# Token loads ahead of stores, a third block convolved on TensorE, and a softmax on eight partitions, in a causal convolution followed by a GELU feed-forward layer

## The chip, the cores and the metric

The kernel runs on one core of one Trainium2 chip. The metric is the device time of that core in microseconds (us), the median of several executions. All other times are taken from one execution recorded by the hardware profiler, counted from the start of its span.

The engines are named as in the profile: PE (TensorE, matrix multiplication; PEld is its loading of weights), DVE (VectorE), ACT (ScalarE), POOL (GpSimd) and SP (SyncE, which here only issues DMA).

## The reference

Two steps are computed one after the other. First a causal convolution of 7 taps along the sequence, with softmaxed taps, one set for each of 8 heads of 24 channels; then a feed-forward layer with an exact GELU.

```python
# x: (8, 4096, 192); weight: (8, 7); w_in: (192, 2048); w_out: (2048, 192)
w = softmax(weight, axis=-1)                      # max subtracted, 1e-9 added to the sum
x_pad = concatenate([zeros((B, 6, D)), x], axis=1)
x_unf = x_pad[:, idx, :].reshape(B, S, 7, 8, 24)  # 7 shifted copies
conv = einsum('hk,bskhg->bshg', w, x_unf).reshape(B * S, 192)
h = conv @ w_in
out = (0.5 * h * (1 + erf(h / sqrt(2)))) @ w_out  # (32768, 192), float32
```

## The kernel before

The 32768 tokens are split into two halves of 16384. Partitions 0 to 63 hold 64 channels of a token of the first half, partitions 64 to 127 the same channels of a token of the second half; `NP` = 3 parts p make up the 192 channels. A block n is `WS[n]` tokens of each half: four blocks of 256 and thirty of 512, so `NB` = 34.

A block passes through these stages:

- **Load** (`load`, L171): four DMAs (q = 0 to 3) bring fp32 tokens into one of three buffers `xin`. A buffer is reused only when all transposes of the block that used it are done (`S_TR`). 380 KB a DMA for a block of 512, 188 KB for one of 256.
- **Transpose** (`trans`, L396) on DVE, into `xT`, which is used in turn by even and odd blocks. POOL (`halo`, L289, L300, L306) adds the tokens that lie ahead of the block.
- **Convolution.** For blocks 2 and up it is done on DVE (`conv`, L419 and L426): 7 taps for each of 3 parts, 21 operations. For the first `ND` = 2 blocks it is done on PE (`pconv`, L575): the tokens are cast to bf16 in `xTb`, then multiplied with 7 diagonal matrices `dg` (made by `diag`, L357), 14 small matmuls a part, into PSUM at the place that `CONVB` names. The result is copied to `xc` by ACT for block 0 (L501) and by DVE for block 1 (`conv_out`, L382).
- **Expansion** `mm1` (L611) on PE, into `hp`, in 8 slices (block of 256) or 16 slices (block of 512); the GELU (L522) on ACT follows each slice.
- **Contraction** `mm2` (L643) on PE into `ob`. Its units for block n-1 are laid between the slices of `mm1` of block n, in equal shares. With 256 tokens a block has 2 groups g, with 512 it has 4; a group has 32 units.
- **Eviction** `evac` (L435) on DVE, from `ob` to `osb`, one for each group, and **store** (L185, L208) by SP.

PE's order is written out by hand (L659 to L679): in block 0 the list `behind` puts extra work behind slices, the three remaining `dup` (which mirror `w_in` into the other half of the partitions, through PE and a DVE copy, L367) and then the three parts of `pconv(1)`. Block n may begin `mm1` only when `xc` is complete (`S_PCE` for the blocks convolved on PE, `S_CV` for the others).

DVE's order is written out too: softmax and diagonals, `trans(0)`, copies of `dup`, `trans(1)`, its casts and copies, and from block 2 on 24 operations a block: 3 transposes, then 21 convolution operations. The table `late` tells ahead of which operation each eviction is placed: `(1, 1): (4, 6)` is group 1 of block 1, ahead of operation 6 of block 4.

SP's queue is in order (L682 to L696): weights of the convolution, loads of blocks 0 to 2 (block 1 only after the first part of `w_in` is there), a wait for `w_out`, then in turn `load(n + 2)` and `store(n - 1)`. A store waits for the evictions of its block, so the load behind it in the queue waits with it.

The softmax (L316 to L352) is computed on all 128 partitions with a broadcast copy of the weights: reduce, subtract on DVE, Exp on ACT, then sum, add, reciprocal, multiply on DVE, and a product with the mask `msk` (made by POOL) and a reduction, which give `wcol`, the tap of each partition. PE meanwhile runs 22 matmuls on zeros (L535), to keep busy until the first data are there.

Of the kernel before, what the change touches and what calls it, by code (L numbers as in the profile page):

```python
# [5 lines left out]
ALU = mybir.AluOpType  # L6
# [5 lines left out]
def bass_lightweight_conv__then__act_gelu_exact_kernel(  # L12
# [21 lines left out]
    ND = 2  # L34
# [54 lines left out]
    with es:  # L89
        win = sbt("win", [128, NP * F], BF16)  # L90
        wout = sbt("wout", [128, NF * C], BF16)
        wsb = sbt("wsb", [128, H * KS], F32)
        wmx = sbt("wmx", [128, H], F32)
        wsm = sbt("wsm", [128, H], F32)
        wrc = sbt("wrc", [128, H], F32)
        wex = sbt("wex", [128, H * KS], F32)
        wnm = sbt("wnm", [128, H * KS], F32)
        msk = sbt("msk", [128, NP * H], F32)
        wpr = sbt("wpr", [128, NP * KS * H], F32)
        wcol = sbt("wcol", [128, NP * KS], F32)  # L100
        idn = sbt("idn", [128, 64], F32)
# [3 lines left out]
        hot = sbt("hot", [128, 2], F32)  # L105
# [15 lines left out]
        S_MSK = sem("S_MSK")  # L121
        S_IDN = sem("S_IDN")
        S_WARM = sem("S_WARM")
# [22 lines left out]
        CONVB = [(ob[0], 0), (ob[0], 512), (ob[1], 0)]  # L146
# [18 lines left out]
        def load(e, n, qs=(0, 1, 2, 3)):  # L165
            mb = WS[n] // 32
            if n >= NX:
                e.wait_ge(S_TR, NP * (n - NX + 1))
            for q in qs:
                off = ((q // 2) * HALF + OFF[n]) * D + 32 * (q % 2)  # L170
                e.dma_start(  # L171
                    ap(
                        xin[n % NX],
                        32 * q * (TB // 32 * D),
                        [[TB // 32 * D, 32], [1, mb * D - 32]],
                    ),
                    ap(xt, off, [[mb * D, 32], [1, mb * D - 32]]),
                ).then_inc(S_XIN[n % NX], 16)
# [43 lines left out]
        def _(g):  # L222
# [8 lines left out]

            g.memset(msk[:, :], 1.0).then_inc(S_MSK)
            g.memset(idn[:, :], 1.0).then_inc(S_MSK)
            g.wait_ge(S_MSK, 2)
            for hf in range(2):
                m = msk[64 * hf : 64 * hf + 64, :]
                g.affine_select(
                    out=m,
                    in_=m,
                    compare_op=ALU.is_ge,  # L240
                    fill=0.0,
                    base=0,
                    pattern=[[64, NP], [-GRP, H]],
                    channel_multiplier=1,
                ).then_inc(S_MSK)
            g.wait_ge(S_MSK, 4)
            for hf in range(2):
                m = msk[64 * hf : 64 * hf + 64, :]
                g.affine_select(
                    out=m,  # L250
                    in_=m,
                    compare_op=ALU.is_ge,
                    fill=0.0,
                    base=GRP - 1,
                    pattern=[[-64, NP], [GRP, H]],
                    channel_multiplier=-1,
                ).then_inc(S_MSK)
            for hf in range(2):
                m = idn[64 * hf : 64 * hf + 64, :]
                g.affine_select(  # L260
                    out=m,
                    in_=m,
                    compare_op=ALU.is_equal,
                    fill=0.0,
                    base=0,
                    pattern=[[-1, 64]],
                    channel_multiplier=1,
                ).then_inc(S_IDN)
            g.wait_ge(S_IDN, 2)
            g.tensor_copy(idb[:, :], idn[:, :]).then_inc(S_IDN)  # L270
# [39 lines left out]

            for n in range(NB):
                halo(n)

        @block.vector
        def _(v):
            v.memset(warm[:, :], 0.0).then_inc(S_WARM)  # L316
            hk = [[H * KS, 128], [KS, H], [1, KS]]
            v.wait_ge(S_WSB, 16)
            v.tensor_reduce(  # L319
                wmx[:, :], ap(wsb, 0, hk), mybir.AxisListType.X, ALU.max, negate=True  # L320
            ).then_inc(S_PRO)
            v.wait_ge(S_PRO, 1)
            v.tensor_tensor(
                ap(wex, 0, hk), ap(wsb, 0, hk), ap(wmx, 0, [[H, 128], [1, H], [0, KS]]), ALU.add
            ).then_inc(S_PRO)
            v.wait_ge(S_ACTP, 2)
            v.tensor_reduce(
                wsm[:, :], ap(wnm, 0, hk), mybir.AxisListType.X, ALU.add
            ).then_inc(S_PRO)
            v.wait_ge(S_PRO, 3)  # L330
            v.tensor_scalar(wsm[:, :], wsm[:, :], 1e-9, None, ALU.add).then_inc(S_PRO)
            v.wait_ge(S_PRO, 4)
            v.reciprocal(wrc[:, :], wsm[:, :]).then_inc(S_PRO)
            v.wait_ge(S_PRO, 5)
            v.tensor_tensor(
                ap(wex, 0, hk), ap(wnm, 0, hk), ap(wrc, 0, [[H, 128], [1, H], [0, KS]]), ALU.mult
            ).then_inc(S_PRO)
            v.wait_ge(S_PRO, 6)
            v.wait_ge(S_MSK, 6)
            v.tensor_tensor(  # L340
                ap(wpr, 0, [[NP * KS * H, 128], [KS * H, NP], [H, KS], [1, H]]),
                ap(wex, 0, [[H * KS, 128], [0, NP], [1, KS], [KS, H]]),
                ap(msk, 0, [[NP * H, 128], [H, NP], [0, KS], [1, H]]),
                ALU.mult,
            ).then_inc(S_PRO)
            v.wait_ge(S_PRO, 7)
            v.tensor_reduce(
                wcol[:, :],
                ap(wpr, 0, [[NP * KS * H, 128], [H, NP * KS], [1, H]]),
                mybir.AxisListType.X,  # L350
                ALU.add,
            ).then_inc(S_PRO)  # L352
            v.wait_ge(S_PRO, 8)
            v.wait_ge(S_IDN, 3)

            def diag(p):
                v.tensor_tensor(  # L357
                    ap(dg, p * KS * 64, [[NP * KS * 64, 128], [64, KS], [1, 64]]),
                    ap(idn, 0, [[64, 128], [0, KS], [1, 64]]),
                    ap(wcol, p * KS, [[NP * KS, 128], [1, KS], [0, 64]]),  # L360
                    ALU.mult,
                ).then_inc(S_DG)
# [16 lines left out]
            def conv_out(n, p):  # L379
                v.wait_ge(S_PC, NP * n + p + 1)  # L380
                b, o = CONVB[p]
                v.tensor_copy(  # L382
                    xc[n % 2][:, p * TB : p * TB + WS[n]], ap(b, o, [[1024, 128], [1, WS[n]]])
                ).then_inc(S_PCE)
# [65 lines left out]
            for p in range(NP):  # L450
                diag(p)
            for p in range(NP):
                trans(0, p)
            for q in range(3):
                dup_out(q)
            for p in range(NP):
                trans(1, p)
            for p in range(NP):
                cast(1, p)
            dup_out(3)  # L460
            for p in range(NP):
                conv_out(1, p)


            late = {(0, 0): (2, 18), (0, 1): (3, 8), (1, 0): (3, 20), (1, 1): (4, 6)}
            late.update({(2, 0): (4, 13), (2, 1): (4, 21)})
            for n in range(3, NB):
                for g in range(NG[n]):
                    b, o = n + 2, len(ops0) * (g + 1) // (NG[n] - 1)
                    if g == NG[n] - 1:  # L470
                        b, o = n + 3, 0
                    late[n, g] = (b, o)
# [10 lines left out]
        def _(a):  # L483
            a.wait_ge(S_WARM, 1)
            a.activation(out=hot[:, 0:1], in_=warm[:, 0:1], func=AF.Exp).then_inc(S_ACTP)
            load(a, 0, (2, 3))
            a.wait_ge(S_ACTP, 1)
            a.wait_ge(S_PRO, 2)
            a.activation(out=wnm[:, :], in_=wex[:, :], func=AF.Exp).then_inc(S_ACTP)
            a.activation(out=hot[:, 1:2], in_=warm[:, 0:1], func=AF.Gelu).then_inc(S_HOT)  # L490
# [7 lines left out]
            for p in range(NP):  # L498
                a.wait_ge(S_PC, p + 1)
                b, o = CONVB[p]  # L500
# [31 lines left out]
        def _(t):  # L532
            t.wait_ge(S_WARM, 1)
            for i in range(22):
                t.matmul(hp[1][:, 0:512], warm[:, 0:128], warm[:, :])  # L535

            def dup(s):

                if s == 0:
                    t.wait_ge(S_IDN, 3)  # L540
# [18 lines left out]
            def pconv(n, p):  # L559
                w = WS[n]  # L560
                b, o = CONVB[p]
                t.wait_ge(S_CAST, NP * n + p + 1)
                t.wait_ge(S_HALO, HC[n] + 2 + p)
                if n == 0:
                    t.wait_ge(S_DG, p + 1)
                elif p == 0:
                    t.wait_ge(S_DUPE, 3)
                elif p == 2:
                    t.wait_ge(S_DUPE, 4)
                for k in range(KS - 1, -1, -1):  # L570
# [19 lines left out]
            behind = {1: [(dup, 1)], 2: [(dup, 2)], 3: [(dup, 3)]}  # L590
            for p in range(NP):
                behind[4 + p] = [(pconv, 1, p)]
# [28 lines left out]
            def mm2(m, g, ph, i):  # L621
# [4 lines left out]
                if i == 0:  # L626
                    if ph == 0:
                        if gg >= 2:
                            t.wait_ge(S_EV, gg - 1)
                    else:  # L630
# [28 lines left out]
            for n in range(NB):  # L659
                todo = units(n - 1) if n >= 1 else []  # L660
                for i in range(NSL[n]):
                    mm1(n, i)
                    if n == 0:
                        for f, *q in behind.get(i, []):
                            f(*q)

                    i0 = 1 if n == 1 else 0
# [14 lines left out]
        def _(sp):  # L682
            sp.dma_start(wsb[:, :], ap(wt, 0, [[0, 128], [1, H * KS]])).then_inc(S_WSB, 16)
            load(sp, 0, (0, 1))
            sp.wait_ge(S_WIN[0], 32)
            load(sp, 1)
            load(sp, 2)
            sp.wait_ge(S_WOUT, 16)
            for n in range(1, NB):
                if n + 2 < NB:  # L690
                    load(sp, n + 2)
# [33 lines left out]
```

## Time and profile before

| | us |
|---|---|
| time, median of 3 runs | 707.97 |
| lowest and highest | 707.60, 708.12 |
| span of the profiled execution | 706.7 |
| PE busy | 687.9 (97%) |
| PEld busy | 521.2 (74%) |
| DVE busy | 558.5 (79%) |
| ACT busy | 528.4 (75%) |
| POOL busy | 39.0 (6%) |
| PE, `mm1` (L611), 3264 matmuls | 422.1 |
| PE, `mm2` (L643), 8192 matmuls | 426.7 |
| ACT, GELU (L522), 512 instructions | 523.0 |
| DVE, fused convolution operations (L426), 480 into `acc` | 316.9 |

Busy times of matmuls overlap, as matmuls of the two row halves run at the same time, so the rows of PE add up to more than its busy time. A busy share is an average over the whole span; what a stage waits for has to be read from the timeline of that stage. The idle time that a row gives is that of the engine ahead of the instruction, with what released it.

### The profile page before, as it was taken

How to read it: one execution, taken by the hardware profiler on the slowest of the kernel's cores; microseconds unless marked ns; L12 is line 12 of the kernel's file. 1: busy time of each engine (PE TensorE's matmuls, PEld its weight loads, DVE VectorE, ACT ScalarE, POOL GpSimd, SP SyncE). 2: the span in 40 equal slices, each digit the busy share in tenths (PEclk: the TensorE clock that was granted, in tenths of full speed). 3: DMA queues.
4: the chain of work that ended last, by engine and by line, in shares of the span. 5: the costliest groups of instructions: out<-in, count | busy, mean ns of one | idle time of the engine just before them, and what ended most of it. 6: DMA issues, size and time to landing. Idle time of an engine off the chain costs nothing.

```text
span 706.7 us, 25342 instructions
## 1 busy us (share of the span) xinstructions
PE 687.9 (97%) x11586; PEld 521.2 (74%) x11586; DVE 558.5 (79%) x924; ACT 528.4 (75%) x523; POOL 39.0 (6%) x90
## 2 busy tenths in 40 slices
PE   6995999999999999999999999999999999999998
PEld 3784677777777777777777777777777777777777
DVE  3879889888889888888988888988888988888811
ACT  4664977777777777777777777777777777777771
POOL 4100000000000000000000000000000000000000
PEclk9998999999999999999999999999999999999999
DMA  9456345554445554335554444565444555434113
GB/s 185 89 118 152 76 98 136 135 118 95 91 103 136 135 132 101 92 87 129 135 135 99 109 86 113 135 135 129 96 92 91 134 135 135 109 90 89 30 46 92
DMA packets 22795, 78.18 MB, mean 111 GB/s; under 512 B 7072, under 2 KB 10912, under 8 KB 18848
## 3 DMA queue, kind: packets, MB, share of 16 engines
q1 hardware_dynamic: 19056, 74.21, 45.7%
q0 software_dynamic: 2896, 1.57, 1.7%
q8 instruction: 91, 1.49, 1.0%
q10 hardware_dynamic: 736, 0.78, 0.4%
q14 instruction: 16, 0.13, 0.1%
HBM read 52.95 MB, written 25.17 MB: 111 GB/s over the span
## 4 chain that ended last, share of the span: by engine, by line
PE 92%; DVE 5%; DMA 2%; issue 1%; SPq 0%; ACT 0%; ACTq 0%
PE ob L643 46%; PE hp L611 45%; DVE acc L426 2%; DMA xin<-in_x_dram 1%; PE ob L575 1%; DVE xT L396 1%; DMA wsb<-in_weight_dram 1%; DVE acc L419 1%; DVE xc L426 0%; DVE osb L435 0%; DVE dg L357 0%; SPq L185 0%; SPq L171 0%; DVE win L367 0%; PE ob L551 0%
## 5 line engine op out<-in xcount | busy, mean ns | idle before, releaser
L522 ACT ACTIVATE gT<-hp 128x1024 bf16<-128x1024 f32 x512 | 523.0, 1023 | 155.6 <-PE hp L611 155.6
L643 PEld LDWEIGHTS ob<-wout,gT 64*128 64x128 bf16 x8192 | 363.9, 94 | 106.5 <-issue 2.5
L611 PE MATMUL hp<-xc,win 64*128 64x512 bf16 (+1 forms) x3264 | 422.1, 365 | 9.7 <-DVE xc L426 7.6
L643 PE MATMUL ob<-wout,gT 64*128 64x192 bf16 x8192 | 426.7, 243 | 1.5 <-issue 1.4
L426 DVE SCALAR_TENSOR_TENSOR acc<-xT,wcol,acc 128x512 f32<-128x512 f32 (+1 forms) x480 | 316.9, 722 | 0.0
L611 PEld LDWEIGHTS hp<-xc,win 64*128 64x128 bf16 x3264 | 161.3, 94 | 65.6 <-issue 9.4
L435 DVE COPY osb<-ob 128x384 f32<-128x384 f32 x128 | 70.2, 548 | 125.5 <-PE ob L643 125.5
L396 DVE STREAM_TRANSPOSE xT<-xin 128x512 f32<-128x512 f32 (+1 forms) x102 | 61.0, 649 | 4.5 <-DMA xin<-in_x_dram 4.5
L426 DVE SCALAR_TENSOR_TENSOR xc<-xT,wcol,acc 128x512 bf16<-128x512 f32 (+1 forms) x96 | 64.5, 723 | 0.0
L419 DVE TENSOR_SCALAR acc<-xT,wcol 128x512 f32<-128x512 f32 (+1 forms) x96 | 55.3, 628 | 1.1
L306 POOL COPY xT<-xT 128x558 f32<-128x558 f32 x32 | 20.9, 652 | 601.7 <-DVE xT L396 601.7
L289 POOL COPY xT<-xT 128x18 f32<-128x18 f32 x29 | 11.5, 396 | 0.0
L575 PE MATMUL ob<-xTb,dg 64*64 64x256 bf16 x84 | 6.8, 321 | 2.8 <-ACT xTb L493 2.5
L575 PEld LDWEIGHTS ob<-xTb,dg 64*64 64x64 bf16 x84 | 5.2, 126 | 4.4 <-ACT xTb L493 3.0
L535 PE MATMUL hp<-warm 128*128 128x512 bf16 x22 | 6.3, 454 | 1.3 <-DVE warm L316 1.3
L367 DVE CAST win<-ob 128x768 bf16<-128x768 f32 x3 | 2.9, 952 | 4.3 <-PE ob L551 4.3
L535 PEld LDWEIGHTS hp<-warm 128*128 128x128 bf16 x22 | 2.4, 114 | 4.6 <-issue 1.9
L501 ACT ACTIVATE xc<-ob 128x256 bf16<-128x256 f32 x3 | 1.1, 383 | 2.6 <-PE ob L575 2.6
L319 DVE TENSOR_REDUCE wmx<-wsb 128x8 f32<-128x56 f32 x1 | 0.2, 211 | 3.6 <-DMA wsb<-in_weight_dram 3.6
L382 DVE CAST xc<-ob 128x256 bf16<-128x256 f32 x3 | 1.3, 419 | 2.2 <-PE ob L575 2.2
L493 ACT ACTIVATE xTb<-xT 128x256 bf16<-128x256 f32 x3 | 1.1, 417 | 2.4 <-DVE xT L396 2.4
L367 DVE CAST win<-hp 128x768 bf16<-128x768 f32 x1 | 1.0, 957 | 2.4 <-PE hp L551 2.4
(35 smaller groups left out, 20.4 us busy)
## 6 DMA issues: line engine op xcount, KB each, us to landing
xin<-in_x_dram SPq DMA_DIRECT2D x120, 380.0 KB, 7.1
out_dram<-osb SPq DMA_DIRECT2D x116, 192.0 KB, 3.0
xin<-in_x_dram SPq DMA_DIRECT2D x14, 188.0 KB, 6.4
out_dram<-osb SPq DMA_DIRECT2D x40, 48.0 KB, 1.7
wout<-in_moe_w_out_dram POOLq DMA_DIRECT2D x1, 768.0 KB, 15.6
win<-in_moe_w_in_dram POOLq DMA_DIRECT2D x2, 288.0 KB, 5.4
out_dram<-osb ACTq DMA_DIRECT2D x8, 48.0 KB, 2.1
xin<-in_x_dram ACTq DMA_DIRECT2D x2, 188.0 KB, 4.9
```

The source lines that it names most:

```text
L289: g.tensor_copy(dst, ap(xT[(n - 1) % 2], WS[n - 1] + 31, [[NP * XW, 128], [XW, NP], [32, HB]],),).then_inc(S_HALO)
L306: g.tensor_copy(ap(t, 1, [[NP * tw, 128], [tw, NP], [32, HB], [1, 31]]), ap(t, WS[n], [[NP * tw, 128], [tw, NP], [32, HB], [1, 31]]),).the ...
L367: v.tensor_copy(ap(win, FH + s * FQ, [[NP * F, 128], [F, NP], [1, FQ]]), ap(DUPB[s], 0, [[1024, 128], [FQ, NP], [1, FQ]]),).then_inc(S_DUPE)
L396: v.transpose(ap(xT[n % 2], p * XW + HL, [[NP * XW, 128], [1, w]]), ap(xin[n % NX], 64 * p, [[TB // 32 * D, 128], [D, w // 32], [1, 32]],) ...
L419: ins = v.tensor_scalar(a, src, wk, None, ALU.mult)
L426: ins = v.scalar_tensor_tensor(dst, src, wk, a, op0=ALU.mult, op1=ALU.add)
L435: v.tensor_copy(ap(osb[m % 2], g * C, [[8 * C, 128], [4 * C, 2], [1, C]]), ap(ob[(G0[m] + g) % 2], 0, [[1024, 128], [512, 2], [1, C]]),).t ...
L522: a.activation(out=ap(gT[n % 2], i * c * 2 * w, dst), in_=ap(hp[u % 2], 0, src), func=AF.Gelu,).then_inc(S_GELU)
L535: t.matmul(hp[1][:, 0:512], warm[:, 0:128], warm[:, :])
L575: ins = t.matmul(b[r, o : o + w], dg[r, d0 : d0 + 64], xTb[n][r, x0 : x0 + w], start=(k == KS - 1), stop=(k == 0), tile_position=(64 * hf, ...
L611: ins = t.matmul(hp[u % 2][:, hf * TB + cc * w : hf * TB + cc * w + w], win[r, p * F + wcols(hf, f0) : p * F + wcols(hf, f0) + 128], xc[n ...
L643: ins = t.matmul(ob[gg % 2][:, 512 * sub : 512 * sub + C], gT[m % 2][r, c0 : c0 + 128], wout[r, CH[i] * C : (CH[i] + 1) * C], start=(ph == ...
```

## The change

There are three parts.

**Loads ahead of stores.** SP issues the load of block 3 at the start (it waits only until block 0 is transposed), no longer waits for `w_out`, and then alternates `load(n + 3)` with `store(n - 1)`. So each load stands ahead of one more store than before. Half of the load of block 1 is issued by ACT. The order of the four DMAs of a load becomes 0, 2, 1, 3.

**Block 2 convolved on PE.** `ND` becomes 3. `pconv(2, p)` is placed behind slices 1, 2 and 3 of block 1; the contraction of block 0 begins at slice 2 rather than 1. The PSUM places of block 2 are all in `ob[1]`, with waits for the copies that free them. DVE casts and copies block 2 rather than convolving it. The evictions of blocks 0 to 3 get new places.

**Softmax on eight partitions.** One partition holds one head, the weights are loaded once (8 x 7). Exp takes the maximum as its bias and gives the sum as well; the table load of Exp is issued at the start as before, on one partition. The taps are then brought to 128 partitions by three small fp32 matmuls with a selection matrix `sel`, made by POOL from a memset of DVE, and copied from PSUM to `wcol`. The zero matmuls become 5 ahead of these and 8 behind. The third diagonal moves behind the transposes of block 0.

```diff
-    ND = 2
+    ND = 3
...
-        CONVB = [(ob[0], 0), (ob[0], 512), (ob[1], 0)]
+        CONVB = [
+            [(ob[0], 0), (ob[0], 512), (ob[1], 0)],
+            [(ob[0], 0), (ob[0], 512), (ob[1], 0)],
+            [(ob[1], 0), (ob[1], 512), (ob[1], 256)],
+        ]
...
+            g.wait_ge(S_MSET, 2)
+            pat = [[64, NP], [0, 2], [1, 64]]
+            g.affine_select(out=sel[:, :], in_=sel[:, :], ...)
+            g.wait_ge(S_SEL, 1)
+            g.affine_select(out=sel[:, :], in_=sel[:, :], ...)
...
+            v.memset(sel[:, :], 1.0).then_inc(S_MSET)
+            v.memset(idb[:, :], 1.0).then_inc(S_MSET)
             v.wait_ge(S_WSB, 16)
             v.tensor_reduce(
+                wmx[:, :], wsb[:, :], mybir.AxisListType.X, ALU.max, negate=True
             ).then_inc(S_PRO)
             v.wait_ge(S_ACTP, 2)
+            v.tensor_scalar(wsm[:, :], wsm[:, :], 1e-9, None, ALU.add).then_inc(S_PRO)
+            v.wait_ge(S_PRO, 2)
+            v.reciprocal(wrc[:, :], wsm[:, :]).then_inc(S_PRO)
+            v.wait_ge(S_PRO, 3)
+            v.tensor_scalar(wnm[:, :], wex[:, :], wrc[:, 0:1], None, ALU.mult).then_inc(S_PRO)
+            v.wait_ge(S_PEP, 1)
+            v.tensor_copy(wcol[:, :], ob[0][:, 0 : NP * KS]).then_inc(S_PRO)
...
-            for p in range(NP):
-                diag(p)
+            diag(0)
+            diag(1)
             for p in range(NP):
                 trans(0, p)
+            diag(2)
             for q in range(3):
                 dup_out(q)
-            for p in range(NP):
-                trans(1, p)
-            for p in range(NP):
-                cast(1, p)
-            dup_out(3)
-            for p in range(NP):
-                conv_out(1, p)
+            for n in range(1, ND):
+                for p in range(NP):
+                    trans(n, p)
+                for p in range(NP):
+                    cast(n, p)
+                if n == 1:
+                    dup_out(3)
+                for p in range(NP):
+                    conv_out(n, p)
...
-            late = {(0, 0): (2, 18), (0, 1): (3, 8), (1, 0): (3, 20), (1, 1): (4, 6)}
-            late.update({(2, 0): (4, 13), (2, 1): (4, 21)})
-            for n in range(3, NB):
+            late = {(0, 0): (3, 4), (0, 1): (3, 14), (1, 0): (4, 1), (1, 1): (4, 9)}
+            late.update({(2, 0): (4, 16), (2, 1): (4, 23), (3, 0): (5, 14), (3, 1): (6, 1)})
+            for n in range(4, NB):
...
+            a.activation(
+                out=wex[:, :],
+                in_=wsb[:, :],
+                func=AF.Exp,
+                bias=wmx[:, 0:1],
+                accum_out=wsm[:, 0:1],
+            ).then_inc(S_ACTP)
+            a.activation(out=hot[:, 1:2], in_=warm[0:1, 0:1], func=AF.Gelu).then_inc(S_HOT)
+            load(a, 1, (2, 3))
...
-            for i in range(22):
-                t.matmul(hp[1][:, 0:512], warm[:, 0:128], warm[:, :])
+            spin(5)
+            t.wait_ge(S_SEL, 2)
+            t.wait_ge(S_PRO, 4)
+            for p in range(NP):
+                ins = t.matmul(
+                    ob[0][:, p * KS : (p + 1) * KS],
+                    sel[:, p * 128 : (p + 1) * 128],
+                    wnm[:, :],
+                )
+            ins.then_inc(S_PEP)
+            spin(8)
...
+                elif n == 2 and p == 0:
+                    t.wait_ge(S_PCE, 2 * NP)
+                elif n == 2 and p == 2:
+                    t.wait_ge(S_PCE, 2 * NP + 1)
...
-                behind[4 + p] = [(pconv, 1, p)]
+                behind[0, 4 + p] = [(pconv, 1, p)]
+                behind[1, 1 + p] = [(pconv, 2, p)]
...
+                        elif gg == 1:
+                            t.wait_ge(S_PCE, NP * ND)
...
-                    i0 = 1 if n == 1 else 0
+                    i0 = 2 if n == 1 else 0
...
-            sp.dma_start(wsb[:, :], ap(wt, 0, [[0, 128], [1, H * KS]])).then_inc(S_WSB, 16)
+            sp.dma_start(wsb[:, :], ap(wt, 0, [[KS, H], [1, KS]])).then_inc(S_WSB, 16)
             load(sp, 0, (0, 1))
             sp.wait_ge(S_WIN[0], 32)
-            load(sp, 1)
+            load(sp, 1, (0, 1))
             load(sp, 2)
-            sp.wait_ge(S_WOUT, 16)
+            load(sp, 3)
             for n in range(1, NB):
-                if n + 2 < NB:
-                    load(sp, n + 2)
+                if n + 3 < NB:
+                    load(sp, n + 3)
                 store(sp, n - 1)
```

## The prediction

> **What bounds the kernel now.** I read the page first: time 707.97 us, profiled span 706.7 us, PE busy 97%, and in section 5 three causes of PE idle. Then the waits of PE between 15 and 110 us, from the start of the first real matmul into the regular part:
>
> ```profile
> PE hp L611 <- DVE xc L426: 7.6, 1, 7.6
> PE ob L643 <- issue: 1.4, 1, 1.4
> PE hp L611 <- DVE win L367: 1.1, 1, 1.1
> ```
>
> Columns: total us, times, longest. From 100 us on, the wait view has no PE entry at all. So nothing done after about 86 us can be gained there; the question is when PE reaches the regular part. The timeline of PE shows the hole:
>
> ```profile
> 50.12 0.66 PE L643 MATMUL ob<-wout,gT 64*128 64x192 bf16 x12
> 52.17 0.34 PE L643 MATMUL ob<-wout,gT 64*128 64x192 bf16 x4 [1.39 <-issue]
> ...
> 58.91 0.83 PE L611 MATMUL hp<-xc,win 64*128 64x256 bf16 x12
> 59.57 0.84 PE L643 MATMUL ob<-wout,gT 64*128 64x192 bf16 x16
> 68.05 1.46 PE L611 MATMUL hp<-xc,win 64*128 64x512 bf16 x6 [7.64 <-DVE xc L426]
> 69.28 0.87 PE L643 MATMUL ob<-wout,gT 64*128 64x192 bf16 x8
> 69.92 1.51 PE L611 MATMUL hp<-xc,win 64*128 64x512 bf16 x6
> 71.20 0.87 PE L643 MATMUL ob<-wout,gT 64*128 64x192 bf16 x8
> 71.84 1.07 PE L611 MATMUL hp<-xc,win 64*128 64x512 bf16 x6
> ```
>
> Block 3 ends near 60.3, block 4 begins at 68.05, and its first slices take 1.87, 1.92 and 1.23 us where the later ones take 0.98. The same timeline for DVE says why block 4 was late:
>
> ```profile
> 45.10 1.27 DVE L426 SCALAR_TENSOR_TENSOR xc<-xT,wcol,acc 128x256 bf16<-128x256 f32 x3
> 50.90 1.90 DVE L396 STREAM_TRANSPOSE xT<-xin 128x512 f32<-128x512 f32 x3 [4.53 <-DMA xin<-in_x_dram]
> ```
>
> DVE stood 4.53 us waiting for the tokens of block 4; without it block 4 would still be about 3 us late, since DVE had two whole 256-wide convolutions before it. The chain of waits goes store, load, transpose: the load of block 4 is queued on SP behind store(0), whose last eviction is at 39.03; its DMA runs from 42.77 to 50.87.
>
> The front, from the timeline of the first 20 us:
>
> ```profile
> 4.85 0.21 DVE L319 TENSOR_REDUCE wmx<-wsb 128x8 f32<-128x56 f32 x1 [3.65 <-DMA wsb<-in_weight_dram]
> 7.53 1.70 DVE L357 TENSOR_TENSOR dg<-idn,wcol 128x448 bf16<-128x448 f32 x3
> 9.14 1.09 DVE L396 STREAM_TRANSPOSE xT<-xin 128x256 f32<-128x256 f32 x3
> 10.09 1.82 PE L575 MATMUL ob<-xTb,dg 64*64 64x256 bf16 x22 [2.54 <-ACT xTb L493]
> 14.52 1.48 PE L611 MATMUL hp<-xc,win 64*128 64x256 bf16 x24 [0.48 <-ACT xc L501]
> ```
>
> The order is weight, softmax, diagonals, transposes, TensorE convolution; the first expansion matmul is at 14.52.
>
> [...] the granted clock is 0.50 from 66 to 72 us and 1.00 before and after. [...] The page has 91 instruction packets and 1.49 MB, 16.4 KB each; the 1.39 us stall "issue" begins at 50.78, as the 8.1 us burst of token loads ends[...]. [...] The DMA share is near or above 0.9 from 4 to 22 us, so an earlier load there delays others.
>
> **The front, step by step.** The weight load shrinks from 28 KB to 224 bytes on eight partitions. Its 4.02 us to landing is the upper bound; the 48 KB stores land in 1.7 us, the lower. I take 2.2, so arrival at about 3.0 instead of 4.83. Behind it: reduce 0.25, Exp with bias and sum 0.35 (row L489 0.25; the added sum is not shown, 0.25 to 0.6), then add, reciprocal and multiply 3 x 0.24, three small fp32 matmuls (not shown; 0.3 to 1.2, take 0.7), copy 0.25: 2.3 us, against 2.70 (4.83 to 7.53) before. Two diagonals at 0.57 instead of three: 1.14. The transposes could start at 3.0 + 2.3 + 1.1 = 6.4; the four token loads of block 0, issued by 2.1 with a median of 4.9 to 6.4 to landing, hold that to about 7. That is 2.1 earlier than 9.14. On GpSimd two selects over 384 elements (64x24 takes 0.245, 64x64 0.265, so about 0.45 each) and the two of idb end near 4.3, before the small matmuls need sel near 4.8. The two DVE memsets lie in the wait for the weights. The two load issues put on ACT (0.43 each) lie after the Gelu table load and before the cast. These cost nothing.
>
> But `spin(8)` stands on PE behind the small matmuls. Cold, one takes 0.43, so from 5.2 to 8.6; warm 0.21, to 6.9. I take 8.6 (PE has been idle before it). The convolution of block 0 then starts at 8.6 instead of 10.09, on a clock that is awake: three parts of 0.88 (the warm values at 21 to 25 us) and the first dup at 0.46 are 3.1 us instead of 3.97. With the ACT copy (0.45) the first expansion is at 12.2 instead of 14.52: 2.3 gained, bounds 1.0 and 3.5.
>
> **Blocks 0 to 3.** PE took 11.5 us from first expansion to block 1 (26.0) and 11.6 more to block 2 (37.63). Added: pconv(2), 3 x 0.88 = 2.65 us, on PE's path. Block 1 starts at 23.7, block 2 at 38.0 (12.2 + 11.5 + 11.6 + 2.65), a little later than before. New waits: pconv(2,p) waits for DVE casts (23.5 + transposes 1.1 + cast 0.3, ready at 25.0, PE comes at 25.7); pconv(2,2) waits for the copy of part 0 (done 27.1, PE comes at 29.6); group 1 of mm2 waits for all copies, long done. wout is first used near 28, its 768 KB landed at 21.8; load 3 adds 752 KB to that stretch, at about 200 GB/s up to 3.8 us: 25.6, still hidden.
>
> DVE loses the nine-microsecond convolution of block 2 (26.90 to 35.84 less one eviction, 8.7) and gains casts 0.86 and copies 1.25, but must wait for PE at the copies; it ends them at 31.1 and begins block 3 then, not at 35.84. Block 3 is 1.1 + 8.7 plus two evictions of 0.47, each of which waits about 0.4 for its PE group: done at 42.6, PE needs it at 48.5.
>
> Tokens of block 4: the load now waits only for trans(1), near 18.6, and lands by about 30 (1.5 MB at 200 GB/s behind the rest); needed at 42.6. The 4.53 us are gone. Load 5 goes out after store(0), near 40, and is needed at 60. Its burst meets PE's dense 256-wide blocks as the old one did.
>
> DVE in block 4: transposes 1.9, multiplies 1.75, then 18 fused operations of 0.67, and four evictions, is about 17.5 us: 60.1. But the last eviction, (2,1), is placed ahead of the last operation and needs the end of PE's block 3: 48.5 + 10.5 = 59.0. Then 0.5 + 0.7 + release: block 4 opens on PE at 60.5, a wait of 1.5 us instead of 7.6, too short for the clock to drop (before, it was granted 1.00 until 64 us, four after PE stopped). If the instruction stall of 1.4 comes back, PE ends at 60.4 and block 4 opens at 61.9.
>
> Block 4 warm is 16 x 0.98 = 15.7; DVE's block 5 is 15.52 (67.82 to 83.34) plus one eviction 0.47 = 16.0 from the same instant. Block 5 starts at 76.5, or 77.9 with the stall. Before: 85.77. The gain is 9.3 or 7.9. It is kept: after block 5 PE takes 20.9 us a block and DVE some 17.5. From there on the load, issued one block earlier by number, is still queued after the previous store, and DVE had no DMA wait there: worth nothing.
>
> Sum: 7.64 of wait to 1.5 (6.1), 2.1 of cold clock, 1.4 of stall perhaps, front 2.3, less 2.65 of added convolution, and small differences. 707.97 - 8.6, the middle of the two, is **699.4 us**.
>
> **Rivals.**
> (a) Likeliest, 0.65: as above, 697.5 to 701.5.
> (b) Less, 0.18: wout or the weights arrive late, or DVE's block 3 waits longer for PE's convolution copies; a wait of 2 to 6 us stays ahead of block 4. For it: DMA is saturated early, and DVE has under 1 us of slack at several evictions. Against: tokens of block 4 have 12 us of slack. About 703.5.
> (c) More, 0.08: warm spins and no stall give 3.5 at the front: 707.97 - 10.5 = 697.5 down to 696.
> (d) Slower, 0.06: two loads now stand queued[...]. For it: the 1.39 us stall. Against: none after 100 us, under the same 1.5 MB bursts. If 30 blocks lost 0.35 each: +10.5 against -8.6, 709.9.
> (e) No change, 0.03: front lost to the added 2.65 and the wait for block 4 replaced by an eviction wait.
>
> **Numbers.** Range 696 to 704: takes (a), (c), most of (b), the front's bounds of 1.2 either way and the stall. Faster 0.91, same 0.03, slower 0.06.
>
> **What would show it.** Right: first expansion near 12, no DVE wait on xin before block 4, PE's wait ahead of block 4 at 1 to 2 us with DVE xc as its releaser, warm first slices, block 5 near 77, and the same 621 us from there to the end. Wrong: a PE wait on wout or on DVE copies near 25 to 31 us, a start of DVE's block 3 after 34, cold slices in block 4, or "issue" stalls after 100 us.

## The result, and the profile after

The changed kernel takes 701.35 us (median of 4 runs, 699.99 to 703.15), the kernel before 707.91 (4 runs): a ratio of 0.9909 with a 95% interval of 0.9882 to 0.9936, so 6.6 us or 0.9% faster. The profiled execution has a span of 698.3 us where the one before had 706.7. Two further sets of the same code gave 700.44 (beside 708.87) and 700.6 (beside 708.91). The forecast was 699.4, range 696 to 704.

The waits of PE between 15 and 110 us, changed kernel (total us, times, longest):

```profile
PE hp L616 <- DVE xc L403: 1.6, 2, 1.4
PE hp L616 <- DVE win L344: 1.1, 1, 1.1
PE hp L616 <- ACT gT L509: 0.4, 1, 0.4
...
```

The wait for `xc` ahead of block 4 went from 7.6 to 1.4 us; a second one of 0.16, ahead of block 5, makes up the 1.6. The 1.4 us stall named "issue" is not there. The timeline of PE where the hole was:

```profile
58.49 0.82 PE L616 MATMUL hp<-xc,win 64*128 64x256 bf16 x12
59.15 0.82 PE L650 MATMUL ob<-wout,gT 64*128 64x192 bf16 x16
61.38 0.82 PE L616 MATMUL hp<-xc,win 64*128 64x512 bf16 x6 [1.41 <-DVE xc L403]
62.02 0.51 PE L650 MATMUL ob<-wout,gT 64*128 64x192 bf16 x8
62.35 0.83 PE L616 MATMUL hp<-xc,win 64*128 64x512 bf16 x6
...
77.36 0.82 PE L616 MATMUL hp<-xc,win 64*128 64x512 bf16 x6 [0.16 <-DVE xc L403]
```

Block 4 opens at 61.38 instead of 68.05. Its first slice takes 0.97 us (61.38 to 62.35), where it took 1.87: the clock stayed up (granted 1.00 from 60 to 68 us, where before it was 0.50 from 66 to 72). Block 5 opens at 77.36 instead of 85.77, which is 8.41 earlier, and the span is 8.4 shorter. Nothing was gained or lost after block 5.

DVE ahead of block 4, same view:

```profile
42.22 1.27 DVE L403 SCALAR_TENSOR_TENSOR xc<-xT,wcol,acc 128x256 bf16<-128x256 f32 x3
43.41 0.70 DVE L373 STREAM_TRANSPOSE xT<-xin 128x512 f32<-128x512 f32 x1
...
58.58 1.40 DVE L403 SCALAR_TENSOR_TENSOR xc<-xT,wcol,acc 128x512 bf16<-128x512 f32 x2
60.01 0.56 DVE L412 COPY osb<-ob 128x384 f32<-128x384 f32 x1
60.49 0.74 DVE L403 SCALAR_TENSOR_TENSOR xc<-xT,wcol,acc 128x512 bf16<-128x512 f32 x1
```

The transpose of block 4 no longer waits for its tokens. The eviction at 60.01 stands between DVE's last two operations of block 4. It needs the end of PE's block 3, which came at 59.97, and DVE was there at 59.98: neither waited for the other. So its 0.56 us are only a part of the remaining 1.4 us; the rest is DVE's own work, which ends that much after PE's block 3 (the first experiment on the evictions shows 0.8 us without it).

The front, timeline of the first 20 us:

```profile
2.23 0.15 DVE L317 TENSOR_REDUCE wmx<-wsb 8x1 f32<-8x7 f32 x1 [0.56 <-DMA wsb<-in_weight_dram]
...
3.97 1.44 PE L529 MATMUL ob<-wnm,sel 8*128 8x7 f32 x6 [0.40 <-POOL sel L247]
...
5.34 3.59 PE L523 MATMUL hp<-warm 128*128 128x512 bf16 x8
...
6.74 1.09 DVE L373 STREAM_TRANSPOSE xT<-xin 128x256 f32<-128x256 f32 x3
...
8.87 2.25 PE L579 MATMUL ob<-xTb,dg 64*64 64x256 bf16 x22
...
12.70 1.48 PE L616 MATMUL hp<-xc,win 64*128 64x256 bf16 x24 [0.48 <-ACT xc L488]
```

The transposes are done from 6.74 rather than 9.14, but PE is in its eight zero matmuls until 8.9, some 0.44 us each, and the convolution starts only behind them.

### The profile page after: what moved, and what is told of

It reads as the page before. It is cut to its first block, busy times and chain, and to the rows that moved or that the text cites. A ratio compares the mean times of both kernels' runs of the same rounds, so it can differ in the third digit from the quotient of the medians.

```text
span 698.3 us, 25401 instructions
## 1 busy us (share of the span) xinstructions
PE 689.0 (99%) x11625; PEld 528.7 (76%) x11625; DVE 551.5 (79%) x908; ACT 529.0 (76%) x524; POOL 39.5 (6%) x87
## 3 DMA queue, kind: packets, MB, share of 16 engines
q0 software_dynamic: 2896, 1.57, 1.6%
q8 instruction: 91, 1.49, 0.9%
## 4 chain that ended last, share of the span: by engine, by line
PE 96%; DVE 3%; issue 1%; POOL 0%; ACT 0%; POOLq 0%; DVEq 0%
PE ob L650 48%; PE hp L616 46%; DVE acc L403 1%; PE ob L579 1%; PE hp L523 1%; DVE xT L373 0%; DVE xc L403 0%; DVE acc L396 0%; PE ob L529 0%; POOL win L229 0%; DVE osb L412 0%; ACT gT L509 0%; DVE win L344 0%; PE ob L551 0%; POOL sel L237 0%
## 5 line engine op out<-in xcount | busy, mean ns | idle before, releaser
L650 PEld LDWEIGHTS ob<-wout,gT 64*128 64x128 bf16 x8192 | 367.7, 94 | 100.0 <-PE ob L650 0.6
L403 DVE SCALAR_TENSOR_TENSOR acc<-xT,wcol,acc 128x512 f32<-128x512 f32 (+1 forms) x465 | 311.1, 733 | 0.0
L616 PEld LDWEIGHTS hp<-xc,win 64*128 64x128 bf16 x3264 | 165.0, 94 | 57.3 <-ACT gT L509 4.3
L579 PE MATMUL ob<-xTb,dg 64*64 64x256 bf16 x126 | 9.1, 291 | 0.3 <-DVE xTb L351 0.3
L579 PEld LDWEIGHTS ob<-xTb,dg 64*64 64x64 bf16 x126 | 6.8, 116 | 2.8 <-issue 1.1
L296 POOL CAST xTb<-xT 128x186 bf16<-128x186 f32 x9 | 3.4, 384 | 14.6 <-DVE xT L373 14.6
```

The costliest lines, as they stand in the source:

```text
L403: ins = v.scalar_tensor_tensor(dst, src, wk, a, op0=ALU.mult, op1=ALU.add)
L579: ins = t.matmul(b[r, o : o + w], dg[r, d0 : d0 + 64], xTb[n][r, x0 : x0 + w], start=(k == KS - 1), stop=(k == 0), tile_position=(64 * hf, ...
L616: ins = t.matmul(hp[u % 2][:, hf * TB + cc * w : hf * TB + cc * w + w], win[r, p * F + wcols(hf, f0) : p * F + wcols(hf, f0) + 128], xc[n ...
L650: ins = t.matmul(ob[gg % 2][:, 512 * sub : 512 * sub + C], gT[m % 2][r, c0 : c0 + 128], wout[r, CH[i] * C : (CH[i] + 1) * C], start=(ph == ...
```

## The experiments

Two questions were left by the result. Which of the three parts brings the 7 to 8 us, and why do runs of the changed kernel differ by 3 us, at a granted clock of 0.999 to 1.000 in all four?

### Each part alone

Loads only: SP, ACT and the order of the four DMAs as in the changed kernel, the rest as before. (That order, and ACT's half of block 1, were not tried apart from the loads.)

```diff
...
             load(sp, 2)
-            sp.wait_ge(S_WOUT, 16)
+            load(sp, 3)
             for n in range(1, NB):
-                if n + 2 < NB:
-                    load(sp, n + 2)
+                if n + 3 < NB:
+                    load(sp, n + 3)
                 store(sp, n - 1)
```

> Only the loads are moved ahead of the stores, the rest as before. Theory (the token load queued behind the store made DVE late for block 4): the 4.53 us wait of DVE on xin before block 4 is gone, block 4 opens on PE at 63.5 instead of 68.05, PE is idle 3.2 us there and the clock drops little or not; block 5 opens at 79 to 81 instead of 85.77; time 701.5 to 703.5. Rival (DVE has two whole convolutions before block 4, so the DMA wait only overlaps with waits on evictions): block 4 opens after 66, time above 705.5.

Measured: 708.99 us (703.3 to 711.04 over 12 runs), ratio 0.9995 (0.9973 to 1.0017). No gain by the median, although DVE's wait on `xin` is gone; two of the 12 runs, 703.30 and 704.94, are near what the theory gave, and no profile of such a run exists. The waits of PE in this kernel, from 10 to 110 us:

```profile
PE ob L644 <- DMA wout<-in_moe_w_out_dram: 5.3, 1, 5.3
PE hp L612 <- DVE xc L426: 3.5, 1, 3.5
...
```

and its timeline of PE:

```profile
25.83 0.83 PE L612 MATMUL hp<-xc,win 64*128 64x256 bf16 x12 [0.44 <-ACT gT L523]
31.92 1.62 PE L644 MATMUL ob<-wout,gT 64*128 64x192 bf16 x18 [5.26 <-DMA wout<-in_moe_w_out_dram]
33.33 1.49 PE L612 MATMUL hp<-xc,win 64*128 64x256 bf16 x12
```

Both theories in the expectation had missed this: a new wait takes the place of the old one. `w_out` now lands at 31.9 instead of 21.8, with the tokens of blocks 3 and 4 moved in the same stretch (with block 3's load behind `w_out`, below, it is back at 21.9). PE stands 5.3 us for it, and its clock is at 0.50 from 32 to 36 us, so the matmuls at 33.33 take 1.49 instead of 0.83. In the changed kernel the same loads do less harm, for two reasons. There `w_out` is in at 24.8 to 27.8 us (three profiles). And `pconv(2)` puts its first use off: it comes 16.0 to 16.3 us behind the first expansion, where it comes 13.4 us behind it in the kernel before.

Convolution only: `ND = 3`, `CONVB`, the places of `pconv(2)` and of the evictions as in the changed kernel; loads and softmax as before.

```diff
-    ND = 2
+    ND = 3
...
+                behind[1, 1 + p] = [(pconv, 2, p)]
...
-                    i0 = 1 if n == 1 else 0
+                    i0 = 2 if n == 1 else 0
```

> Only block 2 is convolved on TensorE, with the new places of the evictions; loads and softmax as before. Theory: DVE is ready for block 4 near 45 but its tokens are still queued behind store(0), so the wait on xin grows from 4.5 to about 6 us and eats what DVE saved; PE is idle some 6 us ahead of block 4 and its clock drops; block 5 opens near 85.7; time 706.5 to 708.5, no gain. Rival (the second convolution on DVE was the cause, not the load): block 4 opens near 63, time 701 to 703.

Measured: 710.47 us, ratio 1.0028 (1.0019 to 1.0036): 0.3% slower than before, a little outside what was expected. The timeline of DVE:

```profile
51.26 0.71 DVE L399 STREAM_TRANSPOSE xT<-xin 128x512 f32<-128x512 f32 x1 [7.40 <-DMA xin<-in_x_dram]
51.89 0.52 DVE L438 COPY osb<-ob 128x384 f32<-128x384 f32 x1
```

and of PE:

```profile
52.47 1.04 PE L655 MATMUL ob<-wout,gT 64*128 64x192 bf16 x16 [1.53 <-DVE osb L438]
...
68.87 1.46 PE L621 MATMUL hp<-xc,win 64*128 64x512 bf16 x6 [4.70 <-DVE xc L429]
```

DVE is ready for block 4 at 43.9 and stands 7.4 us for its tokens. What the convolution gave to DVE went into this wait. It also holds the eviction placed behind the first transpose, and PE waits 1.53 us for that. Block 5 opens at 86.74, a microsecond later than before, although the first expansion is at 13.06 instead of 14.52. Moving work to PE bought nothing while the tokens came late.

Softmax only:

> Only the softmax on eight partitions, its small matmuls, the fewer zero matmuls and the order of the diagonals; loads and convolution as before. Theory: first expansion near 12.7 instead of 14.52, everything behind it shifted by 1.8 including the wait of DVE on xin, which keeps its 4.5 us: time near 706.1, and if the spread of the changed kernel comes from the front, runs differ by 2 us or more. Rival: the shift is lost in the wait ahead of block 4, time 707.5 to 708, spread under 0.6 as before.

```diff
-            sp.dma_start(wsb[:, :], ap(wt, 0, [[0, 128], [1, H * KS]])).then_inc(S_WSB, 16)
+            sp.dma_start(wsb[:, :], ap(wt, 0, [[KS, H], [1, KS]])).then_inc(S_WSB, 16)
...
-            for i in range(22):
-                t.matmul(hp[1][:, 0:512], warm[:, 0:128], warm[:, :])
+            spin(5)
...
+            spin(8)
```

Measured: 708.01 us (706.96 to 709.37), ratio 0.9991 (0.9979 to 1.0003), less than the expected 1.8 us and not clear of zero. In its profile the first expansion is at 11.58, 2.9 us earlier than before, and DVE's wait on `xin` is still 4.8 us. The time is near the rival's, but not for its reason: the shift is not lost in the wait ahead of block 4, since block 5 opens at 83.14, 2.6 us earlier. Of these, 1.1 us are lost behind the last matmul, among the last stores. And the profile of before flatters the front: in three other profiles with the old front (loads only, convolution only, and loads behind `w_out`, below) the first expansion is at 13.06 or 13.07, not at 14.52. There the clock makes the difference. The stretch from 12 to 14 us in the profile of before and in that of loads only (columns: start and end, length, busy time of PE, PEld, DVE, ACT, POOL with counts, then the granted clock, DMA share, GB/s), and the convolution of block 0 in loads only:

```profile
12.00:14.00 2.00, 2.00 (x24) 1.35 (x16) 0.96 (x1) 0.38 (x1) 0.00 (x0) 0.50 1.29 273
12.00:14.00 2.00, 1.52 (x30) 1.16 (x26) 0.90 (x1) 0.69 (x3) 0.00 (x0) 1.00 1.18 241
10.11 1.39 PE L576 MATMUL ob<-xTb,dg 64*64 64x256 bf16 x22 [1.11 <-ACT xTb L494]
```

These first 22 matmuls of the convolution took 1.82 us in the profile of before. With the new front the first expansion was at 11.47 to 12.95, on average 12.4 in eight profiles with eight zero matmuls; with the old one 13.4 in four, or 13.1 without that of before. So the front is worth some 0.7 to 1.0 us, an estimate from these profiles.

The three ratios alone, 0.9995, 1.0028 and 0.9991, add up to 0.14% slower, 1 us; all together the parts give 6.6 to 8.4 us. The gain is not a sum of the three.

### The spread, and w_out

> The changed kernel once more, for its spread (699.99 to 703.15 so far, spans 698.3 to 701.3, where the kernel before spreads over 0.5). Theory A (clock phase): a run of 702 or more shows the clock granted later in the front, first expansion at 14 or later, or a drop after the 1.4 us wait ahead of block 4. Theory B [...]: it shows a stall named issue of 1 us or more between 20 and 90 us. Without either, a profile near 700 and block 5 at 77.4 again.

The unchanged after-kernel again: 700.44 us, 700.10 to 700.79 in four runs, with the first expansion at 12.95 and block 5 at 78.14. No run of 702 turned up, so neither theory was tested. But in this profile `w_out` was in only at 27.8 (issued at 5.7, 22.1 us to landing), and PE first used it at 29.26. After what loads only had shown, that margin of 1.5 us was the new suspect.

> The changed kernel again, as the control for the runs beside it: in two sets its runs went from 699.99 to 703.15 (spans 698.3 to 701.3 at a granted clock of 0.999 to 1.000). Theory (the 768 KB of w_out are crowded by the early loads; they landed at 25.6 and 27.8 in two profiles, and PE first needs them near 29): some runs are 1 us or more above the fastest, at clock 1.000, because w_out landed after 29. Rival [...]: the same spread, and it stays in the kernel that loads block 3 after w_out.

699.32 to 701.14 in five runs, and one of 705.39 at a clock of 0.998; median 700.6. The profiled run was one of the ordinary ones (`w_out` in at 24.8). The long run has the size that a late `w_out` would give, but no profile of it exists.

Block 3's load behind `w_out` again:

```diff
             load(sp, 2)
+            sp.wait_ge(S_WOUT, 16)
             load(sp, 3)
```

> The changed kernel with SP's wait for w_out put back ahead of the load of block 3. Theory: w_out lands near 22, block 3's tokens near 27 (needed at 31.7), block 4's near 34 (needed at 43.4), so nothing waits; the fastest run is as fast as the changed kernel's (699.5 to 700.5) and no run is more than 0.8 above it. Rival [...]: the spread of 2 to 3 us stays.

Measured: 700.33 us (699.46 to 701.03, four runs), ratio to before 0.9879. `w_out` was in at 20.3, and DVE waited for no tokens. The median is that of the changed kernel, and no run is long. Since 3 of 14 runs of the changed kernel are above 702, four runs without one prove little; the spread was 1.6 us, not the 0.8 expected.

The other direction: 752 KB more ahead of block 3's load, into a tile that nothing reads.

```diff
             load(sp, 2)
+            for q in range(4):
+                sp.dma_start(
+                    ap(xx, 32 * q * (TB // 32 * D), [[TB // 32 * D, 32], [1, mb * D - 32]]),
+                    ap(xt, ((q // 2) * HALF + OFF[3]) * D + 32 * (q % 2), [[mb * D, 32], [1, mb * D - 32]]),
+                ).then_inc(S_XX, 16)
             load(sp, 3)
```

> The changed kernel with 752 KB more of tokens loaded ahead of block 3's, into a tile that nothing reads (it adds work and takes none out). Theory (early loads crowd w_out, and its late landing is what makes some runs of the changed kernel 2 us or more longer): at some 200 GB/s that is 3.3 to 3.8 us more, w_out lands at 28.5 to 31.5 instead of 24.8 to 27.8, PE waits up to 2.5 us for it ahead of its first contraction near 29, and the median is 701 to 704 with most runs above 701. Rival (w_out goes at its own pace on the GpSimd queue): it lands before 28 and the time stays at 700.4.

Measured: 707.78 us (706.94 to 708.70, 14 runs), ratio to before 0.9991 (0.9982 to 1.0001): the whole gain is gone. The timeline of PE:

```profile
33.93 1.78 PE L652 MATMUL ob<-wout,gT 64*128 64x192 bf16 x20 [5.01 <-DMA wout<-in_moe_w_out_dram]
35.51 1.49 PE L618 MATMUL hp<-xc,win 64*128 64x256 bf16 x12
...
68.96 0.82 PE L618 MATMUL hp<-xc,win 64*128 64x512 bf16 x6 [1.40 <-DVE xc L405]
```

`w_out` lands at 33.9, 8.3 us later than in the first profile of the changed kernel (6.1 and 9.1 later than in the other two), where the added bytes account for 3.2 to 3.8, an estimate from 237 and 202 GB/s (from 15 to 19 us of the changed kernel, and the first 17 us of its profile). Block 4 opens at 68.96, 7.6 us late: 5.0 of wait and nearly all of the rest slow matmuls behind it (twelve of the expansion take 1.49 us at 35.51 and 0.82 at 39.57). The theory holds in its direction and was too small by half. It shows that early tokens delay `w_out` and by how much PE then pays; that the long runs of the changed kernel are this case is not shown. Two of the three, 702.34 and 703.15, have a granted clock of 1.000, where it is 0.994 to 0.998 here; 705.39 at 0.998 could be such a run. And a spread of 3 us is no mark of the change: the kernel before, in its 47 runs beside the first experiments, one of 902 us left aside, goes from 706.82 to 712.65.

The last piece: loads ahead of the stores, as in loads only, but block 3's load behind `w_out`.

```diff
...
             load(sp, 2)
             sp.wait_ge(S_WOUT, 16)
+            load(sp, 3)
             for n in range(1, NB):
-                if n + 2 < NB:
-                    load(sp, n + 2)
+                if n + 3 < NB:
+                    load(sp, n + 3)
```

> Loads moved ahead of the stores as in the changed kernel, but block 3's load still after w_out; softmax and convolution as before. Theory (the order of loads and stores is worth the 4.5 us wait of DVE, and in the loads-only kernel w_out coming 5.3 us late took it back): no wait on w_out, none of DVE on xin, block 4 opens on PE near 63.5, its first slices are cold for at most one, time 3.5 to 6.5 us under the kernel before beside it. Rival (DVE is late for block 4 anyway): less than 2 us.

Measured: 702.28 us (701.79 to 704.89), ratio 0.9915 (0.9901 to 0.993), 6.6 us under the 708.91 beside it. So this one reordering holds most of what the whole change brings, with the old softmax and block 2 still on DVE. The timeline of PE:

```profile
61.96 1.46 PE L612 MATMUL hp<-xc,win 64*128 64x512 bf16 x6 [3.86 <-DVE xc L426]
```

and the busy time by stretches of 2 us (columns as above):

```profile
60.00:62.00 2.00, 0.04 (x2) 0.07 (x4) 2.00 (x4) 0.00 (x0) 0.00 (x0) 0.74 0.27 71
62.00:64.00 2.00, 2.00 (x16) 1.24 (x18) 1.97 (x4) 0.54 (x1) 0.32 (x1) 0.50 0.70 150
64.00:66.00 2.00, 2.00 (x18) 1.17 (x15) 2.00 (x5) 1.10 (x2) 0.69 (x2) 0.50 1.07 255
```

Here DVE is still late for block 4, by 3.9 us, and in this run the clock drops within that wait and stays down behind it (0.74, 0.50 and 0.50 above; span 701.9 at 0.995; the fastest run has 699.9 at 1.000). With the other two parts as well (the kernel with block 3's load behind `w_out`, above) that wait is 1.4 us. The moved convolution takes work from DVE, and could pay only once the tokens came in time. From first expansion to block 5 it is 67.39 us here and 65.41 there. So the other two parts add some 2 us to this one (700.33 against 702.28, taken side by side); how these divide between them no run shows alone.

### The evictions and the zero matmuls

All from the kernel with block 3's load behind `w_out`.

```diff
-            late.update({(2, 0): (4, 16), (2, 1): (4, 23), (3, 0): (5, 14), (3, 1): (6, 1)})
+            late.update({(2, 0): (4, 16), (2, 1): (5, 0), (3, 0): (5, 14), (3, 1): (6, 1)})
```

> As the kernel that loads block 3 after w_out, with the last eviction of block 2 moved from ahead of the last operation of block 4 to ahead of block 5. Theory: PE's wait ahead of block 4 falls from 1.4 to under 0.4 us, but DVE must then do 16 us of work on block 5 plus that eviction in PE's 15.7, so block 5 opens only 0.5 to 0.8 earlier: time 0.5 to 0.8 lower than that kernel. Rival (the wait is set by PE's own order, not by the eviction): no change, or the wait moves whole to block 5.

699.22 us (698.63 to 700.25), 1.1 below its neighbour, the kernel with block 3's load behind `w_out`. But PE still waits ahead of block 4, and now ahead of block 5 too:

```profile
59.56 0.82 PE L616 MATMUL hp<-xc,win 64*128 64x512 bf16 x6 [0.82 <-DVE xc L403]
...
76.01 0.82 PE L616 MATMUL hp<-xc,win 64*128 64x512 bf16 x6 [0.63 <-DVE xc L403]
```

Together these are 1.45 us, where the neighbour waits 1.40 and 0.16. So the move is worth 0.1 us. The rest of the 1.5 us between the two profiles is what the edit doesn't touch: the first expansion at 11.47 in place of 12.13, and in block 3 of the neighbour's profile a stall of 0.57 us and a little more behind it. DVE's work on block 5 sets the opening of block 5, as the rival half said.

```diff
-            late = {(0, 0): (3, 4), (0, 1): (3, 14), (1, 0): (4, 1), (1, 1): (4, 9)}
-            late.update({(2, 0): (4, 16), (2, 1): (4, 23), (3, 0): (5, 14), (3, 1): (6, 1)})
+            late = {(0, 0): (3, 6), (0, 1): (3, 16), (1, 0): (4, 3), (1, 1): (4, 11)}
+            late.update({(2, 0): (4, 18), (2, 1): (5, 0), (3, 0): (6, 0), (3, 1): (6, 1)})
```

> Block 3's load after w_out, and all evictions of blocks 0 to 3 two operations later, those of (2,1) ahead of block 5 and (3,0) ahead of block 6. Theory (DVE stands 0.5 and 0.6 us for PE ahead of the two evictions of block 0, and its work on block 5 is what opens block 5): these waits and the eviction inside block 5 fall away, PE's waits ahead of blocks 4 and 5 go from 0.8 and 0.6 to under 0.3 each, and from first expansion to block 5 it takes 63.2 to 63.6 instead of 64.5: 1 us lower than the kernel with only the one eviction moved, near 698.3. Rival (PE then waits for these later evictions): a PE wait on osb appears and nothing is gained.

699.29 us (699.13 to 699.87): not below the previous kernel. In the profile the wait ahead of block 4 is gone, the 0.6 ahead of block 5 stays, and first expansion to block 5 is 63.95 us: 0.6 better than with the one eviction moved, not 1. The first expansion was at 12.80 this time, which hides it in the time.

```diff
-            spin(8)
+            spin(5)
```

> The kernel with block 3's load after w_out and the last eviction of block 2 ahead of block 5, with 5 zero matmuls behind the small ones instead of 8. Theory (the zero matmuls hold PE while the data are ready from 7.7): the convolution of block 0 begins at 7.7 instead of 8.5 to 8.9, cold matmuls do work instead of nothing, the first expansion is 0.4 to 0.7 us earlier (11.9 where it was 11.5 to 12.9) and so is the end. Rival (what counts is when the clock comes up): the first matmuls are cold for longer, the first expansion stays between 12 and 13, no gain or a loss.

With one eviction moved: 699.44 us (698.42 to 701.46), first expansion at 11.95; no gain in the time over the 699.22 of the same kernel with eight zero matmuls.

> Both: the evictions as in the tuned kernel, and 5 zero matmuls instead of 8. Theory: the two gains add, 0.4 to 0.7 lower than the tuned kernel, near 697.8. Rival (the zero matmuls only decide when the clock comes up): as the tuned kernel or up to 1 us above it.

With the tuned evictions: 698.18 us (697.93 to 698.97), ratio to before 0.9860 (0.9841 to 0.9879), 1.1 below the tuned kernel. Its front, timeline of PE:

```profile
7.71 2.56 PE L579 MATMUL ob<-xTb,dg 64*64 64x256 bf16 x22
...
11.84 1.48 PE L616 MATMUL hp<-xc,win 64*128 64x256 bf16 x24 [0.48 <-ACT xc L488]
```

The convolution starts at 7.7 when the data are there. Its matmuls are slower (2.56 us for 22, against 2.25), but the first expansion is earlier than in six of the eight profiles with eight zero matmuls. Of the 1.3 us between the spans of this profile and that of the tuned kernel, 0.96 are the first expansion, which spreads by 1.5 us with eight zero matmuls too; so how much the fewer zero matmuls gain by themselves is not shown. This is the fastest version here: 10.0 us under the kernel before beside it, where the changed kernel was 6.6 to 8.4 us under.

## Why the prediction was right, step by step

- **What bounds the kernel.** Right: 8.41 us between the openings of block 5, 8.4 between the spans, no PE wait after.
- **Tokens of block 4.** Right. The 4.53 us wait is gone: they had landed at 30.7, as forecast, and DVE took them up at 43.4.
- **Blocks 0 to 3.** Forecast: block 2 at 38.0, block 3 of DVE at 31.1, PE's block 3 ending at 59.0. Measured 38.77, 31.66 and 59.97. The shifts are those of the first expansion (0.5) and 0.3 in block 1. The added 2.65 us of convolution lies in full on PE's path. One reading was off: 26.90 to 35.84 less an eviction of 0.47 is 8.5 us of convolution on DVE, not 8.7; the waits ahead of the two evictions in block 3, 0.53 and 0.60 instead of 0.4, made up for it.
- **Eviction (2,1) and the wait ahead of block 4.** Forecast 1.5 us, with the clock kept; measured 1.41, clock kept (1.00 from 60 to 68 us). Block 5: 76.5 or 77.9, measured 77.36. The size is right, the releaser only half: the step let DVE wait at that eviction for the end of PE's block 3, but DVE came there no sooner than PE, and with the eviction moved away 0.82 us of the wait were left. That 1.5 us are "too short for the clock to drop" held here, but not as a rule: in convolution only a wait of 1.53 us was followed by a clock of 0.50 (last section).
- **The stall of 1.4.** It was left open, at half its size; it did not come back in the profile of the changed kernel. It isn't gone for good: "issue" stalls of 0.94, 0.55 and 0.51 us stand in loads only, loads behind `w_out` and one of the kernels with five zero matmuls, and in the third profile of the changed kernel PE stands 0.75 us at 50.3, put down to an eviction although the one needed had ended at 45.0. Its cause stays open.
- **The front.** The mechanism was right, the term mis-sized: 2.3 us, with bounds 1.0 and 3.5. Between the two profiles it is 1.8; against the other profiles it is some 0.7 to 1.0. In detail: the weights came sooner than taken (the reduction runs at 2.23, not 3.0), the small matmuls took 1.44 us, above the upper bound of 1.2 (the author's estimate; no matmul of that kind was in the profile of before), and waited 0.4 for POOL's selection matrix, which the step had called free. The zero matmuls ended at 8.9, forecast 8.6. And the step "on a clock that is awake" failed: the first 22 matmuls of the convolution took 2.25 us, slower than the 1.82 before and than the 1.39 of the softmax alone, although the profile has the granted clock at 1.00 from 8 to 12 us.
- **w_out "25.6, still hidden".** It was in at 25.6 in the profile, and hidden, but by luck as much as by design. The step took the added bytes at the mean rate, and the added load showed more than that: 8.3 us later for bytes worth 3.2 to 3.8 (last section). The margin was 1.5 to 4.0 us in three profiles of the changed kernel; with the old front `w_out` came at 31.9, with 752 KB more of tokens at 33.9. Rival (b), a late `w_out`, is what undoes the gain in these two experiments.
- **The size.** 8.6 us forecast. Measured 6.6 in the first set and 8.3 to 8.4 in the two later ones. The first set holds two runs above 702, whose cause was not caught in a profile. That it comes so close has some luck in it: without the stall, as the profile has it, the steps gave 9.3, and 8.4 was measured; the half of a stall in the sum covered the 0.5 us of the first expansion and the 0.3 of block 1.

## What to carry to other kernels

Where several engines take turns being late for the same event, undo the parts one by one before crediting any: here the reordered queue alone gave its time to a wait for `w_out`, and the moved convolution alone gave its time to the wait for tokens that the queue had been keeping. Here tokens that were brought forward moved `w_out` from 21.8 to 31.9 us, and PE waited 5.3 us for it, so write down when each transfer there is first needed, and keep an explicit wait ahead of those that can come later. An order in a queue is worth reading too: here a load behind a store that waits for an eviction cost DVE 4.5 us.

## What was not expected

`w_out`, 768 KB issued from POOL at 5.7 to 6.2 us, landed between 20.1 and 33.9 us, and 752 KB more of tokens pushed it by 8.3 us, twice what their bytes account for. The packets tell more. Between 15 and 19 us of the changed kernel (queue, packets, MB, share of the DMA engines; q1 is SP's, q0 is POOL's, whose 1.57 MB are `w_in` and `w_out`):

```profile
q1 hardware_dynamic: 216, 0.85, 91.4%
q0 software_dynamic: 218, 0.08, 16.9%
```

So in these 4 us the two queues went about packet for packet, and as a packet of q0 carried a tenth of the bytes, `w_out` moved 0.08 MB. The same stretch of the kernel before has 231 packets of q0 to 211 of q1. From 19 to 23 us of the changed kernel, with q1 at 78.4% rather than 91.4% of the DMA engines, it was 618 to 162, and 26 packets of q0 were left. That tokens hold `w_out` back by the number of their packets rather than by their bytes is an estimate from these counts; no run changed the one without the other. In loads only and with the added load `w_out` was in at 31.9 and 33.9: those two are the ones for which PE had to wait.

What a wait of PE cost beyond its own length could not be told from its length here. 3.9 us ahead of block 4 (loads behind `w_out`) left the clock at 0.50 for the next 4 us and more, and 5.0 us for `w_out` became 7.6 at the opening of block 4. But 3.5 us ahead of block 4 in loads only cost nothing more, and the 1.53 us in convolution only, with a stall of 0.20 just ahead, were followed by 3.4 us at 0.50. The stretches behind these two waits, convolution only first (columns as above):

```profile
52.96:56.37 3.41, 3.41 (x44) 2.89 (x40) 3.37 (x7) 1.02 (x1) 1.00 (x2) 0.50 0.24 58
70.10:72.00 1.90, 1.90 (x28) 1.28 (x28) 1.86 (x4) 1.04 (x2) 0.18 (x1) 1.00 0.72 171
```

So the shorter of these two waits was followed by the lower clock. What decides it is not shown.

Two profiles of the same front differ by up to 1.5 us in the first expansion (13.06 and 14.52), with the clock lowered in one of them (0.72, 0.50 and 0.92 in the stretches of 2 us from 10 to 16 us). A gain of 1 us in the front can't be read from one pair of profiles.
